# Arms of the second MoE in another order, without a copy for the last expert, and weight splits on two engines

## The chip, the cores and the metric

The kernel runs on one core of one Trainium2 chip. The metric is the time of one execution on the device in microseconds (us). Engines are named as in the profile: PE is TensorE (PEld its weight loads, PEldq the sequencer that issues them), DVE VectorE, ACT ScalarE, POOL GpSimd, SP SyncE.

## The reference

Three layers run one after the other: a local attention with pooled blocks (2 x 8 heads, 768 positions, 64 wide), a dense MoE with a gated activation (1536 tokens, 512 to 2048 to 512), and a second MoE with 8 experts, which the change concerns:

```python
def _moe2_ref(x, w_gate, w1, w2, capacity):      # capacity = 1536 // 8 * 2 = 384
    logits = x @ w_gate
    expert_idx = np.argmax(logits, axis=1)
    ...                                          # gate_w: softmax weight of that expert
    for i in range(N):                           # first come, first served
        e = expert_idx[i]
        if counts[e] < capacity:
            disp[e, counts[e]] = x[i]
            ...
    h = np.maximum(np.einsum('ecd,edf->ecf', disp, w1), 0.0)   # 512 -> 1024
    y = np.einsum('ecf,efd->ecd', h, w2)                       # 1024 -> 512
    ...                                          # out[i] = gate_w[i] * y[...] or 0
```

Which expert a token takes comes out of the data. For these inputs five of the eight experts have tokens: 878 (of which 384 are kept), 427 (384 kept), 168, 62 and 1. In blocks of 128 tokens that is 3, 3, 2, 1 and 1, ten blocks in all.

## The kernel before

[...]

**The order of the work** is written out by a small planner, `Plan`. Operations are added with an engine, a cost, a due time, and what they read and write; `emit` simulates the engines and writes each engine's instructions in the order that comes out. Among the operations that are ready, the one with the lowest rank goes first, where the rank is 0.67 times the due time less the operation's longest path to the end of the plan (`turn`, L113). One long plan covers everything up to the first block of the second MoE; it is searched with 1200 random variations of the ranks, scored by the planner's own simulation (`tries`, L116 to L125). The plans of the second MoE after that are made once, without a search.

**The experts** are sorted on the device by their number of blocks, the two fullest (of those counted early) first. The first expert's first block lies in the long plan, its second and third come after it. For the expert at place `i` (1, 2, ...) `body(i, nb)` writes the code. `nb` is that expert's number of blocks, a register that each engine reads from a small table (`get_nb`). There are two ways to do an expert's blocks:

- `add_blk`: one block of 128 tokens. First layer: 48 matmuls of 256 columns (L810), ReLU on ScalarE, transposes and splits; second layer: 8 steps of 3 matmuls of 512 columns (L822); scaling (`add_y`) and a scatter to the output by GpSimd (L844).
- `add_pair`: two blocks together (L859, L868), 144 matmuls. A third block, where there is one, follows by `add_blk`.

**While an expert is computed, the next one is prepared** (`more` and `then` in `body`): its token table is loaded (`add_tab`), its tokens are gathered (`add_gather`, L743), transposed and split (`add_prep`), and its weights are split (`add_splits`). The weights come as 8 pieces of 512 KB. Each piece is loaded by SP into a ring of six buffers (`add_stage`, L725), cast to the high part (`split_h`, L731 on ScalarE or L733 on VectorE) and subtracted to the low part (`split_l`, L737). The splits of expert `i + 1` free the ring for the last two pieces of expert `i + 1` and the first six of expert `i + 2`. Of the eight pieces `j`, VectorE casts 2 and 6 and ScalarE the others; GpSimd subtracts 1, 4 and 6 and VectorE the others. GpSimd's work and some of VectorE's take the plan's one `port` in turn.

**The code's shape.** All arms lie in each engine's instruction stream one behind the other, and every engine takes the branches for itself. `body(i)` tests first whether the next expert has a block (L1312). If so, the blocks of expert `i` follow with the preparation of the next, and then `body(i + 1)`, nested within. If not, a second copy of the blocks without any preparation stands in the Else arm, behind all the nested code. In each copy the test of `nb > 1` (L1299) falls through to the code for a pair, behind which the third block stands under `nb > 2` (L1302); the code for one block is the Else arm behind both.

Of the kernel before, what the change touches and what calls it, by code (L numbers as in the profile page):

```python
# [131 lines left out]
def fused_kernel(ctx, tc, qT, kT, vT, vp, w12, wg, wgT, mwe, consts, out, cap=384, dbg=None):  # L132
    nc = tc.nc
    PE, ACT, DVE, POOL, SP = nc.tensor, nc.scalar, nc.vector, nc.gpsimd, nc.sync
# [8 lines left out]
    E = mwe.shape[0]  # L143
# [42 lines left out]
    nblk = CAPR // 128  # L186
# [531 lines left out]
    def xg_at(p, b):  # L718
        return 2 * p + b if b < 2 else 4 + p

    def xs_at(p, b):
        return 2 * p + b % 2

    def stage(i, j, reg, eng=None):
        (eng or SP).dma_start(out=m2["raw"][(8 * i + j) % len(m2["raw"])],  # L725
                     in_=mwe[bass.ds(reg, 1), :, j, :].rearrange("o p f -> (o p) f"))

    def split_h(i, j, eng):
        r, h = m2["raw"][(8 * i + j) % len(m2["raw"])], m2["wh"][i % 2][j]
        if eng is ACT:  # L730
            ACT.activation(out=h, in_=r, func=AF.Copy)  # L731
        else:
            eng.tensor_copy(out=h, in_=r)  # L733

    def split_l(i, j, eng):
        r, h = m2["raw"][(8 * i + j) % len(m2["raw"])], m2["wh"][i % 2][j]
        eng.tensor_tensor(out=m2["wl"][i % 2][j], in0=r, in1=h.bitcast(F32), op=ALU.subtract)  # L737

    def load_tab(t, reg):
        SP.dma_start(out=tabs[t], in_=tab[bass.ds(reg * CAPR, CAPR), :].rearrange("(b p) o -> p (b o)", p=128))  # L740
# [7 lines left out]

    def add_stage(P, i, j, reg, due, eng="Q", r=()):
        P.add(eng, 1.46 if eng == "Q" else .06, due, lambda: stage(i, j, reg(), ENG.get(eng)), r=r,  # L750
              w=[("st", (8 * i + j) % 6)], lat=2.0 if eng == "Q" else 3.5)

    def add_split(P, i, j, due, new=False):
        he = "DVE" if j in (2, 6) else "ACT"
        le = "Pool" if j in (1, 4, 6) else "DVE"
        p, st = i % 2, ("st", (8 * i + j) % 6)

        def h():
            if new:
                wslot(p, j)  # L760
            split_h(i, j, ENG[he])
        hport = ["port"] * (he != "ACT")
        P.add(he, COST[he]["h"], due, h, r=[st], w=[("wh2", p, j)], acq=["wt"] * new + hport, rel=hport)
        P.add(le, COST[le]["l"], due + .5, lambda: split_l(i, j, ENG[le]), r=[st, ("wh2", p, j)], w=[("w", p, j)],
              acq=["port"], rel=["port"])

    def add_splits(P, i, due, gap, cur, nxt, new=False):
        for j in range(8):
            add_split(P, i, j, due + gap * j, new)
            if j < 2:  # L770
                add_stage(P, i, j + 6, cur, due + gap * j)
            elif nxt is not None:
                add_stage(P, i + 1, j - 2, nxt, due + gap * j)

    def add_tab(P, t, reg, due, r=()):
        P.add("Q", .2, due, lambda: load_tab(t, reg()), r=r, w=[("tab", t)])

    def add_gather(P, p, b, t, due, r=()):
        P.add("Pool", 1.04, due, lambda: gather(p, b, t), r=[("tab", t)] + list(r), w=[("xg", xg_at(p, b))], lat=2.5)
# [16 lines left out]
    def add_prep(P, p, b, i, due):  # L796
        g, x = xg_at(p, b), xs_at(p, b)
        add_T(P, lambda: m2["xg"][g], i, lambda: (m2["xh"][x], m2["xl"][x]), due, [("xg", g)], ("xs", x))

    def add_blk(P, p, b, t, due):  # L800
        g, x = xg_at(p, b), xs_at(p, b)

        def l1(j):
            o = m2["hb"][j // 2][:, (j % 2) * 256:(j % 2) * 256 + 256]
            w_h, w_l = m2["wh"][p][j], m2["wl"][p][j]
            n = 0
            for k in range(4):
                ks, ws = slice(k * 128, k * 128 + 128), slice(k * 256, k * 256 + 256)
                for x_, w_ in ((m2["xh"][x], w_h), (m2["xh"][x], w_l), (m2["xl"][x], w_h)):
                    PE.matmul(out=o, lhsT=x_[:, ks], rhs=w_[:, ws], start=n == 0, stop=n == 11)  # L810
                    n += 1

        def relu(i):
            ACT.activation(out=m2["ta"][i], in_=m2["hb"][i], func=AF.Relu)

        def l2(f):
            fs = slice((f % 4) * 128, (f % 4) * 128 + 128)
            g_h, g_l = m2["gh"][f // 4][:, fs], m2["gl"][f // 4][:, fs]
            j, ws = 4 + f // 2, slice((f % 2) * 512, (f % 2) * 512 + 512)
            w_h, w_l = m2["wh"][p][j], m2["wl"][p][j]  # L820
            for n, (g_, w_) in enumerate(((g_h, w_h), (g_h, w_l), (g_l, w_h))):
                PE.matmul(out=m2["acc"][b % 3], lhsT=g_, rhs=w_[:, ws], start=f == 0 and n == 0,  # L822
                          stop=f == 7 and n == 2)

        for j in range(4):
            P.add("PE", 1.43, due + 1.3 * j, lambda j=j: l1(j), r=[("w", p, j), ("xs", x)], w=[("hb", j // 2)])
        for i in range(2):
            P.add("ACT", .6, due + 2.6 * i + 2.6, lambda i=i: relu(i), r=[("hb", i)], w=[("ta", i)])
            add_T(P, lambda i=i: m2["ta"][i], i, lambda i=i: (m2["gh"][i], m2["gl"][i]), due + 2.6 * i + 3.1,
                  [("ta", i)], ("g2", i))  # L830
        for f in range(8):
            P.add("PE", .70, due + 5.2 + .7 * f, lambda f=f: l2(f),
                  r=[("g2", f // 4), ("g2", f // 4, "h"), ("w", p, 4 + f // 2)], w=[("ac", b % 3)])
        add_y(P, p, b, t, due + 11)
# [58 lines left out]
    def wslot(p, j):  # L893
        w = slot("w2", F32R)
        m2["wh"][p][j], m2["wl"][p][j] = w[:, 0, :], w[:, 1, :]

    with tc.manual_schedule():
# [40 lines left out]
        P = Plan(dict(wt=16, raw=3, port=1), dict(Q=1.5, ACT=3, DVE=3, Pool=3, PE=3))  # L938
# [35 lines left out]
        for u in range(NP):  # L974
            hp = u % HP
            (add if u < HP else both)(*(("ACT", .52) if u < HP else ("Pool", .7)), 21 + u + u // HP, lambda u=u: fill_v(u),
                r=[("vs", hp)] + ([("pk", u)] if u < HP else [("pv",)]), w=[("vf", u)])
# [10 lines left out]
        for u in range(NP):  # L988
            hp, b = u % HP, u // HP
# [222 lines left out]
    def get_id(i):  # L1212
        return SP.value_load(rint[0:1, i:i + 1], min_val=0, max_val=E - 1)

    def get_nb(i):
        return nc.values_load(rint[0:1, E + i:E + i + 1], min_val=0, max_val=nblk)
# [36 lines left out]
    with tc.If(m2["full"] > 0) as cmp:  # L1253
        with tc.manual_schedule():
            P = Plan(dict(port=1))
# [6 lines left out]
            nb = get_nb(0)  # L1262
        rest(0, True, nb, 2)
    with cmp.Else():
        with tc.manual_schedule():
            P = Plan(dict(port=1))
# [3 lines left out]
            nb = get_nb(0)  # L1270
        rest(0, False, nb, 1)

    def blocks(i, nb, more=lambda P: None, then=lambda P, due: None):
        p = i % 2

        def one(P):
            more(P)
            add_blk(P, p, 0, i % 4, 0)
            then(P, 9)

        def two(P):
            if nblk > 2:
                add_gather(P, p, 2, i % 4, 3)
            more(P)
            add_pair(P, p, i % 4, 0)
            if nblk > 2:
                add_prep(P, p, 2, 1, 17)
            then(P, 18)

        def plan(fn):  # L1290
            with tc.manual_schedule():
                P = Plan(dict(port=1), dict(ACT=1.9, Pool=1.6))
                fn(P)
                P.emit()

        if nblk == 1:
            plan(one)
            return
        with tc.If(nb > 1) as cmp:  # L1299
            plan(two)  # L1300
            if nblk > 2:
                with tc.If(nb > 2):  # L1302
                    plan(lambda P: add_blk(P, p, 2, i % 4, 0))
        with cmp.Else():
            plan(one)

    def body(i, nb):
        p = i % 2
        if i + 1 < E:
            with tc.manual_schedule():  # L1310
                nx = get_nb(i + 1)
            with tc.If(nx > 0) as cmp:  # L1312
                with tc.manual_schedule():
                    r = get_id(i + 1)
                    q = get_id(i + 2) if i + 2 < E else None

                def more(P):
                    add_tab(P, (i + 1) % 4, lambda: r, 0)
                    for b in range(min(nblk, 2)):
                        add_gather(P, 1 - p, b, (i + 1) % 4, 2 + b)  # L1320
                    add_splits(P, i + 1, 2, 1.2, lambda: r, None if q is None else lambda: q)

                def then(P, due):
                    for b in range(min(nblk, 2)):
                        add_prep(P, 1 - p, b, b, due)
                blocks(i, nb, more, then)
                body(i + 1, nx)
            with cmp.Else():
                blocks(i, nb)
        else:  # L1330
            blocks(i, nb)

    with tc.manual_schedule():
        nb = get_nb(1)
    body(1, nb)


# [77 lines left out]
```

## Time and profile before

| | |
|---|---|
| median of three runs (lowest, highest) | 549.02 us (547.86, 552.17) |
| the profiled execution's own time, its span | 551.83 us, 550.1 us |
| PE busy, DVE, ACT, POOL | 493.9 us (90% of the span), 356.7, 322.4, 112.7 |
| mean granted clock of TensorE | 0.953 |
| first matmul of the second expert after the first one's blocks | 432.55 us |
| last matmul | starts at 542.41 us, 0.40 us long |

Times in the profile are us from the start of the span. [...] A wait is the idle time of an engine just before an instruction, with the instruction or transfer that released it; "issue" stands where the profile shows nothing that was waited for. Branches are no busy time, but they have records with a start and a duration.

### The profile page before, as it was taken

The page shows a single profiled execution, that of the slowest core. Times are in us where ns is not written, and L with a number is a line of the kernel's source. Part 1 is how long each engine was busy: PE and PEld are TensorE (multiplying, and loading weights), DVE is VectorE, ACT ScalarE, POOL GpSimd, SP SyncE. Part 2 cuts the span into 40 slices and gives each one's busy share as a digit, 9 for nine tenths or more (in the row PEclk, how much of TensorE's full clock was granted, in tenths as well). Part 3 has the DMA queues.
Part 4 walks back from the last instruction along what each step waited for, and adds up shares of the span by engine and source line. Part 5 has one row for each costly group of instructions (what it writes and reads, how often), then busy time and mean ns, then how long its engine had stood idle before and what let it go on. Part 6 is the DMA issues. An engine that isn't in the chain of part 4 may idle for free.

```text
span 550.1 us, 9126 instructions
## 1 busy us (share of the span) xinstructions
PE 493.9 (90%) x3360; PEld 435.8 (79%) x3360; DVE 356.7 (65%) x705; ACT 322.4 (59%) x535; POOL 112.7 (20%) x110
## 2 busy tenths in 40 slices
PE   4977689998899999999999999969999999994754
PEld 3767588887788988988889989959888788884553
DVE  5479999999745896885885984445862373462400
ACT  2677788898367676666666655777523433532501
POOL 3450001010241000100101001141522351624400
PEclk9798699999899999999999999989999999996978
DMA  8999869521342532413533206844416672565520
GB/s 304 344 378 411 291 123 144 173 92 51 111 133 89 167 88 91 48 51 96 18 87 49 61 22 117 199 143 154 96 59 192 214 251 75 177 210 182 154 57 6
DMA packets 51587, 78.51 MB, mean 143 GB/s; under 512 B 15491, under 2 KB 34823, under 8 KB 49467
## 3 DMA queue, kind: packets, MB, share of 16 engines
q1 hardware_dynamic: 47850, 68.60, 45.0%
q0 software_dynamic: 2224, 5.47, 3.1%
q10 hardware_dynamic: 1440, 3.54, 1.8%
q8 instruction: 38, 0.62, 0.5%
q14 instruction: 35, 0.28, 0.2%
HBM read 67.39 MB, written 9.99 MB: 141 GB/s over the span
## 4 chain that ended last, share of the span: by engine, by line
PE 57%; DMA 17%; issue 9%; DVE 8%; ACT 5%; SPq 1%; POOL 1%; another core or an unknown queue 0%; POOLq 0%; ACTq 0%; DVEq 0%
PE h L520 18%; PE acc L557 16%; DMA out_dram<-tb,tabs 13%; PE av L452 4%; PE sc L379 4%; PE hb L810 3%; PE acc L822 2%; DMA xg<-x2d,tabs 2%; PE pt L428 2%; DVE wtmp L225 2%; PE avx L557 2%; DMA kraw<-in_kT_dram 1%; PE mx L557 1%; PE hb L859 1%; PE tps L784 1%
## 5 line engine op out<-in xcount | busy, mean ns | idle before, releaser
L520 PE MATMUL h<-xh,ws 128*128 128x256 f32 x768 | 147.1, 286 | 3.5 <-DVE ws L238 2.1
L520 PEld LDWEIGHTS h<-xh,ws 128*128 128x128 f32 x768 | 121.9, 190 | 5.7 <-DVE ws L238 2.3
L557 PE MATMUL acc<-ws,gh 128*128 128x512 f32 x320 | 106.4, 414 | 3.1 <-ACT gh L540 3.1
L520 PE MATMUL h<-xl,ws 128*128 128x256 f32 x384 | 108.8, 283 | 0.0
L520 PEld LDWEIGHTS h<-xl,ws 128*128 128x128 f32 x384 | 73.1, 190 | 0.5
L526 ACT ACTIVATE tA<-h 128x512 f32<-128x512 f32 x48 | 28.4, 594 | 74.3 <-PE h L520 74.3
L557 PEld LDWEIGHTS acc<-ws,gh 128*128 128x128 f32 x320 | 59.0, 194 | 15.4 <-ACT gh L540 3.5
L557 PE MATMUL acc<-ws,gl 128*128 128x512 f32 x160 | 64.8, 405 | 3.0 <-DVE gl L544 3.0
L810 PE MATMUL hb<-w,xh 128*128 128x256 f32 x192 | 39.4, 304 | 16.3 <-issue 11.7
L664 POOL DMA_INDIRECT tab<-toki,ix x12 | 14.1, 1174 | 173.9 <-DVE ix L657 129.8
L810 PEld LDWEIGHTS hb<-w,xh 128*128 128x128 f32 x192 | 32.9, 208 | 18.0 <-issue 17.7
L536 DVE TENSOR_TENSOR tA<-h,tA 128x512 f32<-128x512 f32 x48 | 31.3, 682 | 15.0 <-ACT tA L531 15.0
L557 PEld LDWEIGHTS acc<-ws,gl 128*128 128x128 f32 x160 | 30.9, 193 | 12.0 <-DVE gl L544 4.6
L791 DVE TENSOR_TENSOR gl<-tps,gh 128x512 fp32r<-128x512 f32 x12 | 8.3, 688 | 45.2 <-ACT gh L788 45.1
L544 DVE TENSOR_TENSOR gl<-tA,gh 128x1024 fp32r<-128x1024 f32 x24 | 32.1, 1340 | 7.6 <-PE mx L557 3.0
L607 DVE SCALAR_TENSOR_TENSOR dots<-x,wgb 128x512 f32<-128x512 f32 x48 | 33.4, 695 | 2.0 <-DMA wgb<-in_wgT_dram 1.2
L737 POOL TENSOR_TENSOR w<-mr,w 128x1024 fp32r<-128x1024 f32 x11 | 28.0, 2548 | 32.0 <-ACT w L731 24.2
L737 DVE TENSOR_TENSOR w<-mr,w 128x1024 fp32r<-128x1024 f32 x17 | 28.9, 1703 | 4.5 <-ACT w L731 4.4
L822 PE MATMUL acc<-w,gh 128*128 128x512 f32 x96 | 31.2, 406 | 0.0
L532 ACT ACT_TABLE_LOAD x24 | 30.8, 1283 | 0.4
L529 ACT ACT_TABLE_LOAD x24 | 30.8, 1283 | 0.4
L408 ACT ACTIVATE s<-s,nm 128x120 f32<-128x120 f32 x64 | 24.4, 384 | 9.2 <-POOL vz L358 8.4
(189 smaller groups left out, 1021.7 us busy)
## 6 DMA issues: line engine op xcount, KB each, us to landing
w<-in_w_dram SPq DMA_DIRECT2D x16, 1024.0 KB
mr<-in_mwe_dram SPq DMA_DIRECT2D x28, 512.0 KB
q<-in_qT_dram SPq DMA_DIRECT2D x16, 256.0 KB
kraw<-in_kT_dram SPq DMA_DIRECT2D x8, 400.0 KB
x2d<-x SPq DMA_DIRECT2D x6, 513.0 KB
kw<-in_kT_dram SPq DMA_DIRECT2D x16, 192.0 KB
vw<-in_vp_dram SPq DMA_DIRECT2D x16, 192.0 KB
out_dram<-zer SPq DMA_DIRECT2D x1, 3072.0 KB
```

The source lines that it names most:

```text
L408: ACT.activation(out=s[:, t, :], in_=ps[:, t, :], func=AF.Exp, bias=nm[:, t:t + 1], scale=0.125, accum_out=sm[:, t:t + 1])
L520: PE.matmul(out=o, lhsT=w_, rhs=x_[:, k, :], start=n == 0, stop=n == 3 * HP - 1)
L526: ACT.activation(out=tA[s][:, i * 512:i * 512 + 512], in_=hps[s, i], func=AF.Tanh, scale=0.5)
L529: ACT.preload_act_table_set("trig_and_small")
L532: ACT.preload_act_table_set("exp_and_others")
L536: DVE.tensor_tensor(out=t, in0=hps.pop((s, i)), in1=t, op=ALU.mult)
L544: (POOL if s in GLP else DVE).tensor_tensor(out=gl[s].rearrange("p a b -> p (a b)"), in0=tA.pop(s), in1=gh[s].bitcast(F32).rearrange("p a ...
L557: PE.matmul(out=acc[c][t], lhsT=g_, rhs=w_, start=(ft == 0 and n == 0), stop=(ft == NFT - 1 and n == 2))
L607: DVE.scalar_tensor_tensor(out=rt[c]["ps"], in0=rt[c]["x"][:, t, 0:DM], scalar=1.0, in1=wgb[i][:, j * DM:j * DM + DM], op0=ALU.mult, op1=A ...
L737: eng.tensor_tensor(out=m2["wl"][i % 2][j], in0=r, in1=h.bitcast(F32), op=ALU.subtract)
L810: PE.matmul(out=o, lhsT=x_[:, ks], rhs=w_[:, ws], start=n == 0, stop=n == 11)
L822: PE.matmul(out=m2["acc"][b % 3], lhsT=g_, rhs=w_[:, ws], start=f == 0 and n == 0, stop=f == 7 and n == 2)
```

## The change

Three things. First, every split casts on ScalarE and subtracts on VectorE; this holds for the first two experts too, whose splits are in the long plan. Second, `body` has one copy of the blocks, which always prepares the next expert (unless `i` is the eighth place); the test for a next expert comes behind the blocks. So the last expert that has tokens also prepares an expert without tokens. Third, in that copy the one-block code falls through, and the pair with the third block is the Else arm. Along with that, the one-block arm gathers and prepares one block of the next expert instead of two where `i` is 2 or more, and the due times are lower: 1 + b instead of 2 + b for the next expert's gathers, 4 instead of 9 for the prepares in the one-block arm, 13 instead of 18 in the pair, and 15 instead of 17 for the third block's.

```diff
--- before.py
+++ after.py
@@ -751,8 +751,7 @@
               w=[("st", (8 * i + j) % 6)], lat=2.0 if eng == "Q" else 3.5)
 
     def add_split(P, i, j, due, new=False):
-        he = "DVE" if j in (2, 6) else "ACT"
-        le = "Pool" if j in (1, 4, 6) else "DVE"
+        he, le = "ACT", "DVE"
         p, st = i % 2, ("st", (8 * i + j) % 6)
 
         def h():
@@ -1270,65 +1269,61 @@
             nb = get_nb(0)
         rest(0, False, nb, 1)
 
-    def blocks(i, nb, more=lambda P: None, then=lambda P, due: None):
+    def plan(fn):
+        with tc.manual_schedule():
+            P = Plan(dict(port=1), dict(ACT=1.9, Pool=1.6))
+            fn(P)
+            P.emit()
+
+    def body(i, nb):
         p = i % 2
+        ahead = min(nblk, 2 if i < 2 else 1)
+        nx = r = q = None
+        if i + 1 < E:
+            with tc.manual_schedule():
+                nx = get_nb(i + 1)
+                r = get_id(i + 1)
+                q = get_id(i + 2) if i + 2 < E else None
+
+        def more(P, n):
+            if nx is None:
+                return
+            add_tab(P, (i + 1) % 4, lambda: r, 0)
+            for b in range(n):
+                add_gather(P, 1 - p, b, (i + 1) % 4, 1 + b)
+            add_splits(P, i + 1, 2, 1.2, lambda: r, None if q is None else lambda: q)
+
+        def then(P, due, n):
+            for b in range(n if nx is not None else 0):
+                add_prep(P, 1 - p, b, b, due)
 
         def one(P):
-            more(P)
+            more(P, ahead)
             add_blk(P, p, 0, i % 4, 0)
-            then(P, 9)
+            then(P, 4, ahead)
 
         def two(P):
             if nblk > 2:
                 add_gather(P, p, 2, i % 4, 3)
-            more(P)
+            more(P, 2)
             add_pair(P, p, i % 4, 0)
             if nblk > 2:
-                add_prep(P, p, 2, 1, 17)
-            then(P, 18)
-
-        def plan(fn):
-            with tc.manual_schedule():
-                P = Plan(dict(port=1), dict(ACT=1.9, Pool=1.6))
-                fn(P)
-                P.emit()
+                add_prep(P, p, 2, 1, 15)
+            then(P, 13, 2)
 
         if nblk == 1:
             plan(one)
-            return
-        with tc.If(nb > 1) as cmp:
-            plan(two)
-            if nblk > 2:
-                with tc.If(nb > 2):
-                    plan(lambda P: add_blk(P, p, 2, i % 4, 0))
-        with cmp.Else():
-            plan(one)
-
-    def body(i, nb):
-        p = i % 2
-        if i + 1 < E:
-            with tc.manual_schedule():
-                nx = get_nb(i + 1)
-            with tc.If(nx > 0) as cmp:
-                with tc.manual_schedule():
-                    r = get_id(i + 1)
-                    q = get_id(i + 2) if i + 2 < E else None
-
-                def more(P):
-                    add_tab(P, (i + 1) % 4, lambda: r, 0)
-                    for b in range(min(nblk, 2)):
-                        add_gather(P, 1 - p, b, (i + 1) % 4, 2 + b)
-                    add_splits(P, i + 1, 2, 1.2, lambda: r, None if q is None else lambda: q)
-
-                def then(P, due):
-                    for b in range(min(nblk, 2)):
-                        add_prep(P, 1 - p, b, b, due)
-                blocks(i, nb, more, then)
+        else:
+            with tc.If(nb < 2) as cmp:
+                plan(one)
+            with cmp.Else():
+                plan(two)
+                if nblk > 2:
+                    with tc.If(nb > 2):
+                        plan(lambda P: add_blk(P, p, 2, i % 4, 0))
+        if nx is not None:
+            with tc.If(nx > 0):
                 body(i + 1, nx)
-            with cmp.Else():
-                blocks(i, nb)
-        else:
-            blocks(i, nb)
 
     with tc.manual_schedule():
         nb = get_nb(1)
```

## Rows read from the trace of the kernel before

**Rows 1.** Windows of three stages: each engine's busy us and instructions, clock, DMA share, GB/s.
```profile
0.00:405.00 405.00, 375.81 (x2628) 332.23 (x2629) 303.39 (x633) 274.68 (x460) 64.90 (x79) 0.96 0.52 141
...
432.50:495.00 62.50, 60.86 (x393) 54.05 (x392) 32.42 (x36) 26.40 (x43) 26.93 (x17) 1.00 0.57 178
495.00:528.50 33.50, 16.37 (x90) 14.14 (x88) 10.07 (x12) 10.42 (x14) 13.16 (x8) 0.80 0.54 160
```

**Rows 2.** Waits of TensorE from 380 us on: total us, times, longest us.
```profile
PE hb L810 <- issue: 11.7, 3, 8.5
PE hb L810 <- ACT w L731: 4.6, 1, 4.6
```

**Rows 3.** Timeline of TensorE in the last 50 us: start, duration, idle before and releaser.
```profile
499.82 0.76 PE L810 MATMUL hb<-w,xh 128*128 128x256 f32 x2 [4.58 <-ACT w L731]
...
504.49 0.58 PE L810 MATMUL hb<-w,xh 128*128 128x256 f32 x1 [2.83 <-issue]
...
512.87 0.65 PE L784 MATMUL tps<-ident,ta 128*128 128x128 f32 x4 [1.23 <-ACT ta L814]
...
528.55 0.77 PE L810 MATMUL hb<-w,xh 128*128 128x256 f32 x2 [8.54 <-issue]
```

**Rows 4.** Branches of TensorE's weight-load sequencer, by line: ns min/median/max, first and last start.
```profile
L1299 PEldq COMPARE_BRANCH  x1: 65/65/65, 430.6 to 430.6; - x1
...
L1302 PEldq COMPARE_BRANCH  x1: 286/286/286, 466.8 to 466.8; - x1
...
L1302 PEldq COMPARE_BRANCH  x2: 319/561/803, 492.4 to 495.4; - x2
...
L1299 PEldq COMPARE_BRANCH  x1: 2764/2764/2764, 496.9 to 496.9; - x1
...
L1312 PEldq COMPARE_BRANCH  x1: 5258/5258/5258, 517.1 to 517.1; - x1
...
L1299 PEldq COMPARE_BRANCH  x1: 6004/6004/6004, 522.4 to 522.4; - x1
...
L1299 PEldq COMPARE_BRANCH  x1: 3310/3310/3310, 539.6 to 539.6; - x1
```

**Rows 5.** Windows of four short stretches, with the columns of rows 1.
```profile
364.80:368.30 3.50, 3.48 (x11) 2.95 (x12) 0.69 (x1) 2.33 (x4) 0.22 (x1) 0.52 0.31 119
499.80:508.20 8.40, 5.54 (x24) 5.27 (x25) 0.34 (x1) 0.00 (x0) 4.38 (x4) 0.50 0.86 261
520.00:525.00 5.00, 0.01 (x1) 0.00 (x0) 1.97 (x3) 0.69 (x2) 1.19 (x1) 1.00 0.83 222
528.50:532.20 3.70, 3.65 (x18) 3.68 (x18) 0.00 (x0) 0.00 (x0) 0.00 (x0) 0.52 0.05 13
```

**Rows 6.** Casts and subtractions of the splits: ns min/median/max, first and last start.
```profile
L731 ACT ACTIVATE w<-mr x21: 1038/1059/1069, 352.3 to 514.1; 128x1024 fp32r<-128x1024 f32 x21
...
L737 DVE TENSOR_TENSOR w<-mr,w x17: 1209/1224/3577, 347.5 to 520.2; 128x1024 fp32r<-128x1024 f32 x17
L737 POOL TENSOR_TENSOR w<-mr,w x11: 2359/2404/3259, 354.9 to 515.7; 128x1024 fp32r<-128x1024 f32 x11
```

**Rows 7.** The gathers among the DMA issues: count, median us from issue to landing.
```profile
xg<-x2d,tabs POOLq DMA_INDIRECT x13, 3.9
```

**Rows 8.** Branches of SyncE and GpSimd, and the end of the program: columns as in rows 4.
```profile
L1299 SPq COMPARE_BRANCH  x2: 38/42/45, 528.9 to 531.8; - x2
...
L1299 POOLq COMPARE_BRANCH  x1: 38/38/38, 545.9 to 545.9; - x1
...
L1411 POOLq DRAIN  x3: 46/107/3007, 546.3 to 549.8; - x3
```

**Rows 9.** GpSimd from 350 to 358 us, and a wait of TensorE before 405 us.
```profile
354.90 2.40 POOL L737 TENSOR_TENSOR w<-mr,w 128x1024 fp32r<-128x1024 f32 x1 [14.06 <-ACT w L731]
357.47 1.79 POOL L743 DMA_INDIRECT xg<-x2d,tabs  x1 [0.16 <-issue]
...
PE tps L784 <- DMA xg<-x2d,tabs: 3.8, 1, 3.8
```

## The prediction

> **What bounds the kernel now.** I read the windows first, cut where the stages end. Until 405 us TensorE works on attention, the first MoE and the first block of the second MoE; it is busy for 375.8 of 405 us there, and for 60.9 of 62.5 us in the stretch of the two experts that run as pairs of blocks (432.5 to 495). From 495 to 528.5 it is busy for 16.4 of 33.5 us, at a mean clock of 0.80, and afterwards again nearly without a break [rows 1]. So TensorE is the bound all the way, and the loose time lies where the fourth expert and then the fifth begin.
>
> The waits of TensorE say what this loose time is: 11.7 us in three pieces in which it "waited for nothing that the profile shows", and 4.6 us set down to a ScalarE cast [rows 2]. The order in time places them: 4.58 us before the fourth expert's first matmul at 499.82, 2.83 us within that block, 8.54 us before the fifth's at 528.55 [rows 3]. The branch records of TensorE's weight-load sequencer explain them. A branch that falls through takes 0.065 us (430.6 us); an unconditional jump over the code for one block takes 0.29 (466.8). But the jump over the code of two blocks and the third (to the one-block arm, 496.9) takes 2.76; the two in a row by which the fifth expert gets to its code (first to the copy without a successor, 517.1, then to the one-block arm in it, 522.4) take 5.26 and 6.00; the last one, when all is quiet, 3.31 [rows 4]. 496.9 + 2.76 = 499.7 and 522.4 + 6.00 = 528.4: the first matmuls follow 0.1 us later. So the 4.58 us is a jump too, and not the cast that the waits name.
>
> Each hole costs again through the clock. [...] Busy time there is 5.54 and 3.65 us, of which half, 2.8 and 1.8, is lost. The two transitions thus cost A = 4.6 + 2.8 + 2.8 = 10.2 us and B = 8.5 + 1.8 = 10.3 us.
>
> **The change, part by part.** The profiled execution took 551.83 us, 1.7 more than its span and 2.8 above the median of 549.02. I make the sum in its microseconds and take it off the median.
>
> *A, into the fourth expert.* Before, TensorE's sequencer meets a jump over the third block (0.80, at 492.4), lands at 495.4 on a jump over the one-block code (0.32), and at 496.9 on the one of 2.76. After, only the jump over the third block is left; where it lands, the count is read and two branches fall through. Of the path to 499.82, 2.76 + 0.32 = 3.1 us goes, and the wait becomes 1.5 us. The second hole (2.83) is a wait for the code after the landing, while the DMA engines are 0.86 busy [rows 5]; whether it comes again depends on where the code's blocks lie, so between 0 and 2.83; I take 0.8. Clock: after the 1.23 us wait at 512.87 [rows 3] the matmuls kept the durations of full speed, while the 3.8 us wait before 364.8 [rows 9] cost 3.5 us of half speed [rows 5]; 1.5 us is nearer the first, so 0.5 of the possible 1.8. Left: 2.8, saved 7.4 (ends 4.1 and 10.2).
>
> *B, into the fifth.* Two far jumps become one, at the end of the one-block arm over the code of two blocks and the third; the test of the successor and the test of the count then fall through. Nearest price: 5.26, same place, same moment, DMA engines 0.83 busy from 520 to 525 [rows 5]; ends 2.76 and 6.00. Between the end of the jump at 495.4 and 496.9 lie 1.2 us, in which the next count is read. The jump comes ahead of that reading now, so it starts near 516 and ends at 521.3, and with the reading the first matmul is at 522.5 to 523 instead of 528.55. TensorE ended at 528.55 - 8.54 = 520.0, so 3.0 us of wait stays, with 1.8 of clock and 0.8 for the following code. Left 5.6, saved 4.7 (ends 1 and 10).
>
> *Jumps that are new.* The second and third experts now jump over the one-block code into their arm. For the third this replaces the jump of 0.29 over the same code at 466.8; for the second it is added at 430.6, where TensorE has work until 432.5. At 0.3 it is hidden; at 2.76 it would show 0.9, at 6.0 some 4. I take 0.3. [...]
>
> *Splits.* For each expert ScalarE goes from 6 casts to 8 at 1.06 us (6.4 to 8.5), VectorE from two casts and five subtractions to eight subtractions (8 x 1.22 = 9.8), and GpSimd loses three of 2.40 (7.2). VectorE's subtraction took up to 3.58 where GpSimd worked beside it [rows 6], so VectorE hardly loses. In the pair stage TensorE covers this: 62.5 us hold some 17 us of casts. I take 0.3 for casts that stand in front of a ReLU. In a one-block arm of some 14 us, casts, ReLUs and copies fill ScalarE for 12 to 13 us; the fourth expert already pays 1.23 for two casts in front [rows 3]. I add 0.5 there, and 1.7 for the fifth, which had no splits at all (0 to 3).
>
> *The fifth expert's new work.* It now prepares an expert with no tokens: one table, one gather, eight loads of 512 KB, eight splits, one transposition group. On TensorE those four transposes are paid by the second prepare that the fourth expert drops. The due time of the prepares, 4 for 9, moves their rank in the plan from 3.9 to 0.55 (0.67 x due less the 2.13 of their path), and second-layer step f ranks at -4.16 + 1.17 f: so their transposes move from behind the seventh of eight steps to behind the fifth, about 10.5 us into a block. A gather issued 4 to 5 us in and landing 3.9 us later [rows 7] is there by then: 0. At the end the span outlasts the last matmul by about 7 us, of which GpSimd's drain is 3.0 [rows 8]. GpSimd gets a second jump; its last one, at 545.9, stood 0.4 us ahead of the drain. SP is the risk: behind the fourth expert's loads its own jumps had it at 528.9 and 531.8, 8.9 and 11.8 us after the last matmul of that block [rows 8], and now the same loads lie in front of the end. They start sooner without GpSimd's splits. I take 1.2 (0 to 4).
>
> *The long plan before 405 us* holds the splits of the first two experts, and its order is searched anew at random. One stall there belongs to the change: TensorE waits 3.8 us for a gather, which GpSimd issued at 357.5, right behind a subtraction of 2.40 that is now gone [rows 9]; 2.4 of it and the clock's 1.7 could go, unless the new order takes it back. I take -1.5 (-5 to +4).
>
> Sum: -7.4 - 4.7 + 0.3 + 0.3 + 0.5 + 1.7 + 1.2 - 1.5 = -9.6, so 549.0 - 9.6 = 539.4 us.
>
> **The rivals.** *The number of jumps falls, their price does not.* What TensorE waits for is code behind data in the DMA engines (0.83 to 0.86 busy in both holes), and one jump at 6.00 with a second wait of 2.83 behind it does what two did. Then A saves 4.1, B 1: 549 - 5.1 + 4.0 - 1.5 = 546.4. For it: the 2.83 follows a jump that was already paid. Against: 11.3 us of B are two records that add up.
>
> *Slower: the new order of the long plan.* The search scores its own model, which knows nothing of a gather that lands late. TensorE idles 29.2 us before 405 [rows 1]. If a worse order adds two thirds of this, 19, the rest (-8.1 without the gain there) cannot carry it: 560. It decides from 13.6 us more idle time on, where slower by 1% begins. Against: the same search with as many tries has left only these 29.2 us, those before the first data arrived among them.
>
> *The end grows.* If SP and the fifth expert's loads set the end with 11.8 us after the last matmul where 7 stood, 4.8 instead of 1.2: 543.0, still faster or at the edge of no change.
>
> **How the numbers follow.** A measurement of this kernel can tell about 1%, 5.5 us. Forecast with its spread and the longer end: 0.70; jumps at their old price: 0.21; the worse plan: 0.09. Adding the ends of each term as independent gives -7 and +10 around 539.4; the range is 531 to 549.5, which takes in the second case and leaves out the third and the best corner. Faster 0.69, same 0.22, slower 0.09.
>
> **What would show it.** Between the third and fifth experts the branch records should hold one jump of TensorE over 2 us, not three; the waits without a cause fall from 11.7 to about 5 us; the half-speed stretch after the fourth expert's start is gone. GpSimd has no subtractions, VectorE none over 1.3 us. The fifth block gets a wait for a ReLU of 1 to 2 us. Wrong would make it: the first L810 matmul of the second MoE moved by more than 4 us either way (the plan), a jump of 5 us at 430 or 468, or an end more than 9 us behind the last matmul.

## The result, and the profile after

The changed kernel took 542.16 us (median of four runs, 540.21 to 544.11) against 550.56 of the kernel before beside it; the ratio is 0.987, with a 95% interval of 0.983 to 0.992. In a second session it was 0.988 (0.983 to 0.994). So it is 1.2 to 1.3% faster, 6 to 7 us by these ratios (the two medians lie 8.4 us apart), where 9.6 were forecast. The profiled execution took 540.21 us, 1.95 us below its median, the one of before 551.83, 1.3 above its own: these two flatter the change, and stages tell more than their totals. One execution of one experiment below (mixed splits, 547.72 us) was in a slower state of the chip, and no ratio or median here counts it.

The windows of the fourth and the fifth expert in the changed kernel, cut at the last matmuls of the third, the fourth and the fifth; columns as in rows 1:

```profile
495.10:510.50 15.40, 13.10 (x84) 11.31 (x84) 11.20 (x11) 11.15 (x14) 3.10 (x3) 1.00 0.71 223
510.50:527.30 16.80, 13.23 (x84) 11.25 (x84) 11.19 (x12) 11.14 (x14) 2.82 (x2) 1.00 0.89 290
```

In the 33.5 us in which TensorE was busy for half of the time at a clock of 0.80 [rows 1] there was one block and the way to the next; now 32.2 us (15.40 + 16.80) hold two blocks, at 1.00. TensorE's waits there (rows 3 after):

```profile
496.15 0.48 PE L809 MATMUL hb<-w,xh 128*128 128x256 f32 x2 [1.05 <-ACTq L1322]
503.75 0.66 PE L783 MATMUL tps<-ident,ta 128*128 128x128 f32 x4 [1.23 <-ACT ta L813]
512.69 0.48 PE L809 MATMUL hb<-w,xh 128*128 128x256 f32 x2 [2.22 <-issue]
520.23 0.66 PE L783 MATMUL tps<-ident,ta 128*128 128x128 f32 x4 [1.23 <-ACT ta L813]
```

The 4.58 us became 1.05, the 2.83 is gone, the 8.54 became 2.22, and the fifth block has got the ReLU wait of the fourth. The waits without a cause from 430 us on fall from 11.7 to 3.3 us in all. The branches of TensorE's weight-load sequencer (rows 4 after; L1317 is the test of one block and the jump over its Else arm, L1325 the test of a next expert):

```profile
L1317 PEldq COMPARE_BRANCH  x1: 2836/2836/2836, 428.1 to 428.1; - x1
...
L1317 PEldq COMPARE_BRANCH  x1: 333/333/333, 466.7 to 466.7; - x1
...
L1317 PEldq COMPARE_BRANCH  x2: 68/2076/4085, 507.8 to 512.5; - x2
...
L1317 PEldq COMPARE_BRANCH  x1: 5241/5241/5241, 524.6 to 524.6; - x1
L1325 PEldq COMPARE_BRANCH  x1: 4497/4497/4497, 530.3 to 530.3; - x1
```

Between the third and the fifth expert one jump over 2 us is left, 4.09 (the first of the two in its row). At the end there are two, 5.24 and 4.50, where one of 3.31 was [rows 4].

That a long jump waits for code is read from the same traces, in which one of the DMA queues is named "q8 instruction" (38 packets, 0.62 MB before, 36 and 0.59 MB after). From 425 us on, every branch record of this sequencer over 2 us, in all twelve profiles, overlaps a packet of 16 KB on this queue, and none of the jumps under 1 us does. The record ends 1.0 to 1.9 us behind the last such packet. The second hole of before, from 501.66 to 504.49, holds such a packet too (502.15 to 503.10).

### The profile page after: what moved, and what is told of

Same layout as the page of the kernel before. It is cut to its first block, busy times and chain, and to the rows that moved or that the text cites. A ratio compares the mean times of both kernels' runs of the same rounds, so it can differ in the third digit from the quotient of the medians.

```text
span 538.5 us, 9210 instructions
## 1 busy us (share of the span) xinstructions
PE 487.6 (91%) x3360; PEld 428.3 (80%) x3360; DVE 359.5 (67%) x718; ACT 339.7 (63%) x553; POOL 71.6 (13%) x95
## 5 line engine op out<-in xcount | busy, mean ns | idle before, releaser
L557 PE MATMUL acc<-ws,gh 128*128 128x512 f32 x320 | 104.4, 408 | 3.2 <-ACT gh L540 2.2
L557 PEld LDWEIGHTS acc<-ws,gh 128*128 128x128 f32 x320 | 57.9, 190 | 15.7 <-ACT gh L540 2.6
L737 DVE TENSOR_TENSOR w<-mr,w 128x1024 fp32r<-128x1024 f32 x32 | 38.4, 1220 | 18.5 <-ACT w L731 18.5
L731 ACT ACTIVATE w<-mr 128x1024 fp32r<-128x1024 f32 x32 | 32.8, 1057 | 9.5 <-issue 5.0
L809 PE MATMUL hb<-w,xh 128*128 128x256 f32 x192 | 35.1, 283 | 3.3 <-issue 2.2
L607 DVE SCALAR_TENSOR_TENSOR dots<-x,wgb 128x512 f32<-128x512 f32 x48 | 33.5, 697 | 1.0
L809 PEld LDWEIGHTS hb<-w,xh 128*128 128x128 f32 x192 | 29.6, 189 | 4.5 <-issue 4.1
L544 DVE TENSOR_TENSOR gl<-tA,gh 128x1024 fp32r<-128x1024 f32 x24 | 29.5, 1229 | 4.7 <-PE mx L557 3.7
L531 ACT ACTIVATE tA<-tA,hpi 128x1024 f32<-128x1024 f32 x24 | 27.6, 1152 | 0.8
## 6 DMA issues: line engine op xcount, KB each, us to landing
x2d<-x SPq DMA_DIRECT2D x6, 513.0 KB
```

Source lines behind the costliest of these rows:

```text
L544: (POOL if s in GLP else DVE).tensor_tensor(out=gl[s].rearrange("p a b -> p (a b)"), in0=tA.pop(s), in1=gh[s].bitcast(F32).rearrange("p a ...
L557: PE.matmul(out=acc[c][t], lhsT=g_, rhs=w_, start=(ft == 0 and n == 0), stop=(ft == NFT - 1 and n == 2))
L607: DVE.scalar_tensor_tensor(out=rt[c]["ps"], in0=rt[c]["x"][:, t, 0:DM], scalar=1.0, in1=wgb[i][:, j * DM:j * DM + DM], op0=ALU.mult, op1=A ...
```

## The experiments

For each profile I read five instants off TensorE's timeline: the second expert's first matmul, the last matmul of the third, the fourth and the fifth expert, and the end of the span. The table gives the stretches between them in us (pairs, A, B, tail), their sum, and the ratio of times to the kernel before with its 95% interval.

| | pairs | A | B | tail | sum | ratio |
|---|---|---|---|---|---|---|
| before | 62.7 | 24.8 | 22.8 | 7.3 | 117.6 | |
| changed | 64.1 | 15.4 | 16.8 | 11.2 | 107.6 | 0.987 (0.983 to 0.992) |
| changed, again | 64.1 | 15.3 | 18.4 | 13.0 | 110.8 | 0.988 (0.983 to 0.994) |
| new splits only | 64.0 | 23.8 | 22.5 | 7.2 | 117.5 | 1.002 (0.999 to 1.005) |
| new code only | 62.8 | 15.8 | 19.6 | 12.5 | 110.7 | 0.989 (0.985 to 0.993) |
| no last work | 64.1 | 15.3 | 14.8 | 9.6 | 103.9 | 0.985 (0.981 to 0.989) |
| no far loads | 64.1 | 15.3 | 14.6 | 9.2 | 103.3 | 0.977 (0.972 to 0.981) |
| old order | 64.0 | 23.5 | 15.5 | 11.3 | 114.2 | 1.000 (0.997 to 1.003) |
| copy back | 64.1 | 16.0 | 22.9 | 7.1 | 110.1 | 0.991 (0.988 to 0.994) |
| chain | 64.1 | 17.1 | 15.3 | 12.7 | 109.1 | 0.990 (0.987 to 0.994) |
| mixed splits | 62.8 | 15.3 | 16.9 | 10.7 | 105.7 | 0.989 (0.983 to 0.995) |
| last falls through | 62.8 | 15.9 | 12.6 | 8.5 | 99.8 | 0.968 (0.963 to 0.972) |

What lies before the pairs is not in the sum. It scatters from run to run: the second expert's first matmul came between 430.5 and 437.5 us in these profiles.

**New splits only.** Theories: the gain is the jumps, or it is the splits.

```diff
-        he = "DVE" if j in (2, 6) else "ACT"
-        le = "Pool" if j in (1, 4, 6) else "DVE"
+        he, le = "ACT", "DVE"
```

> Only the splits are moved to ScalarE and VectorE; the arms and the copy for the last expert are those of the kernel before. Theory J (the gain is the jumps): the three jumps of 2.8, 5 and 6 us stay, the long plan before 405 us gives about 1.6 us, the stage of the pairs takes about 1.4 back: 549 to 552 us against 550.6. Rival S (the gain is GpSimd's port given free and the long plan): 545 us or less.

550.26 us beside 548.63: no gain. The holes, now of 4.33, 1.70 and 7.56 us, stand where they stood; the pairs take 1.3 us more. Rival S fell.

**New code only**: the changed kernel with the old two lines of splits put back.

> Only the order of the arms and the copy for the last expert are changed, with their due times; the splits stay on three engines. Theory J: nearly the whole gain, 538 to 543 us, the waits before the fourth and fifth expert at 1 to 3 us, and the first matmul of the second expert at 432.5 us as in the kernel before. Rival S: 546 us or more.

544.03 us. The code alone carries the gain (0.989 against 0.987), and A is that of the changed kernel. B is 2.8 us longer than in the changed kernel's first profile and 1.2 longer than in its second, the tail 1.3 longer than in the first and 0.5 shorter than in the second: the splits' part there is not settled.

**No last work.**

```diff
-            if nx is None:
+            if nx is None or i == 4:
                 return
...
-            for b in range(n if nx is not None else 0):
+            for b in range(n if nx is not None and i != 4 else 0):
```

> The changed kernel, but the fifth expert prepares nothing for the sixth place, which has no tokens here (a kernel that would be wrong for inputs that use six experts). Theory L (the useless loads and splits hold up the last jumps and the end): the end comes 7 us after the last matmul instead of 11, and the 1.2 us wait for a ReLU in the fifth block goes: 5 us less, 537 us. Rival N (the end is set by two far jumps in place of one, whatever is loaded): at most 1.5 us less, 540.5 us or more.

541.74 us, which is N's time. By the stages both theories held half: the fifth block lost its ReLU wait and 2.0 us, and the tail lost 1.6 of the 3.9 us by which it had grown; the jumps behind the fifth block are still 3.82 and 4.30 us without any load, against 5.24 and 4.50. In this profile what lies before the pairs was the slowest of all (437.5 us), and so its time shows less than its stages; whether the other executions were as slow there is not on record.

**No far loads.**

```diff
-            add_splits(P, i + 1, 2, 1.2, lambda: r, None if q is None else lambda: q)
+            add_splits(P, i + 1, 2, 1.2, lambda: r, None if q is None or i in (3, 4) else lambda: q)
```

> The changed kernel without the loads of the six weight pieces for the sixth and seventh place, which the fourth and the fifth expert issue (no tokens there for these inputs; the splits of the sixth place run on what the buffers hold). The same jumps over the same code. Theory D (a far jump waits for code behind data in the DMA engines): the jump behind the fourth block goes from 4.1 to about 2.8 us, the two at the end from 5.2 and 4.5 to about 3.3; the end 8 us behind the last matmul; 538 us. Rival F (a jump costs by its distance): 4.1, 5.2 and 4.5 stay within 0.4, and the time within 1.5 us of 542.

537.33 us, theory D's time; its jump prices only in part:

```profile
L1317 PEldq COMPARE_BRANCH  x2: 68/1656/3245, 508.6 to 512.5; - x2
...
L1317 PEldq COMPARE_BRANCH  x1: 3701/3701/3701, 523.2 to 523.2; - x1
L1325 PEldq COMPARE_BRANCH  x2: 198/2270/4342, 527.4 to 532.1; - x2
```

The same jump behind the fourth block costs 3.25 us in this one profile, and 4.09 to 5.26 in the six that have its loads (changed 4.09, no last work 4.33, mixed splits 4.40, new code only 4.83, copy back 4.89, changed again 5.26); the wait before the fifth expert falls to 0.33. The last one of 4.34 stays. The DMA packets show where the difference lies: the 16 KB packet of the instruction queue starts 0.95 us behind this branch here (509.5), 1.5 us in the changed kernel (509.3), where the weight loads keep the DMA engines 0.93 busy (507.8 to 510.9), and 2.9 us in its second profile (511.6). So a far jump here costs 3.2 to 4.3 us without far loads, and behind the fourth block 0.8 to 2.0 more with them: its code comes later.

**Old order**, and **copy back**: each undoes one half of the new code (the second diff in outline).

```diff
-            with tc.If(nb < 2) as cmp:
-                plan(one)
-            with cmp.Else():
+            with tc.If(nb > 1) as cmp:
                 plan(two)
                 ...
+            with cmp.Else():
+                plan(one)
```

> The changed kernel with the old order of the arms: the pair falls through, the one-block code is the Else arm; still one copy. Theory O (the order of the arms saves what is lost before the fourth expert, the missing copy what is lost before the fifth): from the third expert's last matmul to the fourth's again 24 to 25 us instead of 15.4, from there to the fifth's last matmul 16 to 18 us; at the end one far jump instead of two, so about 2 us less there; 549 us, no gain over the kernel before. Rival M (the missing copy makes most of the gain, the order little): 545 us or less.

```diff
+        with tc.If(nx > 0) as last:
+            blocks()                  # the changed kernel's arms, with more and then
+            body(i + 1, nx)
+        with last.Else():
+            blocks()                  # the same arms without more and then
```

> The changed kernel with a second copy of the blocks, without any preparation, for the last expert, as in the kernel before; the arms in the new order. Theory O: two far jumps in a row before the fifth expert again, the wait there 5 to 7 us instead of 2.2 and half speed after it; the end again 7 to 8 us behind the last matmul instead of 11.2, and no wait for a ReLU in the fifth block: the two sides cancel, 541 to 544 us. Rival P (the second jump costs nothing because the first already hides it, so that the useless preparation is pure loss): 538 us or less. Rival Q (the missing copy is where the gain is): 546 us or more.

548.17 and 544.29 us: theory O held in both but for one point. With the old order A is 23.5 us again and nothing is gained, although the second jump into the fifth expert is gone (B 15.5): the tail of 11.3 and the pairs' 1.3 take their share. The point that failed is this tail: TensorE and GpSimd have one far jump there instead of two, and it is no shorter than the changed kernel's 11.2, so the number of jumps does not set it (what does, see *The end* below). The old order also has the lower due times and the dropped prepare; in A these alone gain no more than 0.3 us (23.5 for the 23.8 of new splits only). With the copy back, these two rows stand ahead of the fifth expert, and the wait there is 7.82 us with half speed behind it (a clock of 0.50 from 520.6 to 524.2), more than expected:

```profile
L1317 PEldq COMPARE_BRANCH  x1: 4885/4885/4885, 510.1 to 510.1; - x1
...
L1328 PEldq COMPARE_BRANCH  x1: 4876/4876/4876, 515.4 to 515.4; - x1
```

The tail is 7.1 in exchange. With the copy in place the order of the arms goes with 0.9% (the new splits in it), and the missing copy with 0.3 to 0.4% on top, which is within the intervals; without the new order the missing copy is worth nothing.

**Chain.** From the fourth expert (place 3) on, one-block code follows one-block code (in outline):

```diff
+        if i == 3:
+            with tc.If(nb < 2) as cmp:
+                plan(one)
+                with tc.If(nx > 0):
+                    body(i + 1, nx, True)      # one-block code only from here on
+            with cmp.Else():
+                ...
```

> The changed kernel; from the fourth place on, where the experts are sorted and none later has more blocks, the one-block code goes on into one-block code for the next places with no Else arm between. The jump behind the fourth expert's block is gone, nothing else. Theory O: the wait of 2.2 us before the fifth expert's first matmul is gone, at the end a jump out of the chain takes the place of the one over the Else arm: 540 us. Rival: the code behind still comes late (a wait of 2 us or more without a jump): 542 us.

The wait before the fifth expert is gone, as expected, and the time is 544.30 us: nothing gained. In its place TensorE waits for gathers inside both blocks, 1.16 and 0.96 us, and the jumps at the end are 5.44 and 4.66. The tail of 12.7 is set by SP this time: its drain (the engine's last step) starts at 541.3, GpSimd's at 535.1. Why the gathers come late was not tried. The first of these waits (start, duration, what it is, and the idle time before it):

```profile
511.48 0.66 PE L783 MATMUL tps<-ident,xg 128*128 128x128 f32 x4 [1.16 <-DMA xg<-x2d,tabs]
```

**Mixed splits.** Old splits up to place 3, new ones from place 4 on:

```diff
         he, le = "ACT", "DVE"
+        if i < 4:
+            he = "DVE" if j in (2, 6) else "ACT"
+            le = "Pool" if j in (1, 4, 6) else "DVE"
```

> The changed kernel with the old splits (VectorE and GpSimd too) for the experts at places 0 to 3 and the new ones from place 4 on. Theory O: from the second expert's first matmul to the third's last 62.7 us instead of 64.1, the fourth and the fifth as in the changed kernel (15.4 and 16.8 us): 541 us. Rival: the old splits cost in the pairs what they cost beside one block, and nothing is gained: 542 us or more.

The pairs are back at 62.8 us, A and B as in the changed kernel. The time, 540.91 us (median of five), is near the 541 expected, but its ratio of 0.989 is no better than the changed kernel's 0.987 and 0.988, with a wide interval: the gain of the pairs doesn't show in it.

**Last falls through.** Mixed splits, and in a chain from place 3 on (in outline):

```diff
+                with tc.If(nx < 1) as last:
+                    plan(one)                  # without more and then
+                with last.Else():
+                    plan(one)                  # with them
+                    body(i + 1, nx, True)
```

> A version for all inputs, put together from the runs before it: old splits for the experts at places 0 to 3, new ones after; from place 3 on a chain of one-block code in which the test for a next expert comes first, the block without any preparation falls through, and the block with preparation is the Else arm, followed by the next place. So the last expert has its own code again, but no far jump leads to it. Theory O, by stage against the changed kernel: pairs 62.8 us (64.1), to the fourth's last matmul 15.5 to 18 (15.4; one jump over one block's code is new), to the fifth's 12.5 to 13.5 (16.8), from there to the end 8.5 to 9.5 (11.2; no useless loads, still two far jumps): 4 to 6 us less, 536 to 538 us. Rival (each jump into code that has not just been run past costs 3 to 5 us, the short one too): the new jump shows as a wait of 3 us with half speed behind it, and the time is 541 us or more.

533.75 us beside 552.56 of the kernel before and 546.16 of the changed one in the same session; it beats both, by more than the 4 to 6 us expected. Its windows of the fourth and the fifth expert:

```profile
493.30:509.20 15.90, 13.03 (x86) 11.68 (x86) 11.11 (x11) 11.28 (x14) 2.60 (x3) 1.00 0.66 218
509.20:521.80 12.60, 12.55 (x81) 10.69 (x79) 1.49 (x3) 3.09 (x5) 1.00 (x1) 1.00 0.34 122
```

The fifth block fills its 12.6 us; the new short jump, over one block's code, cost 0.228 us, and the wait before the fourth block is 1.65 us where it was 1.05, at full speed behind it. At the end one jump of 3.61 and one of 0.19 are left, so the tail came out at the lower end.

**The changed kernel again.**

> The changed kernel once more, beside the version above. Theory O and its rivals alike: 540 to 544 us, 1 to 1.6% under the kernel before; stages as in its first profile to 0.3 us after the second expert's first matmul, whereas that matmul itself may start anywhere from 430 to 438 us.

546.16 us, above the 540 to 544 expected, but the kernel before was slower in that session too (552.56), and 1.16% under it is as expected. The stages were not within 0.3 us: the three far jumps took 5.26, 4.78 and 7.05 us, and the wait of 2.63 before the fifth expert, unlike that of 2.22, had reduced speed behind it (mean clock 0.71 from 514.8 to 518.4). The price of a far jump differs from run to run.

## Why the prediction was right, and where its terms were off

The likeliest case came true: faster by 1.2 to 1.3%, inside the range, by the jumps. That the sum came so near is in part luck: the two transitions gave more than forecast, and the end, the splits in the pairs and the long plan took it back. One of the signs that were to make it wrong did come, an end more than 9 us behind the last matmul (11.2, and 13.0 in the second profile); the other two did not (the first one-block matmul of the second MoE at 380.23 for 383.00, the jump at 428.1 at 2.84). Its terms, by the first profile of the changed kernel:

- *A*, with the added ReLU wait: 7.4 - 0.5 = 6.9 forecast, 9.4 measured. The wait was 1.05 for 1.5, neither the second hole nor half speed came (a clock of 1.00, for 0.50 before [rows 5]), and the ReLU wait stayed at 1.23. The wait was off by a misread row: of the two jumps of L1302 [rows 4], the one at 492.4 took 0.32 and the one that it lands on, at 495.4, 0.80, and I had them the other way round (row below, of before). With 2.76 + 0.80 off the path the same sum leaves 1.0.

```profile
L1302 PEldq COMPARE_BRANCH  x1: 803/803/803, 495.4 to 495.4; - x1
```

- *B*, with the fifth expert's splits: 4.7 - 1.7 = 3.0 forecast, 6.0 measured here and 4.4 in the second profile. The jump took 4.09 for 5.26 (5.26 in the second), the wait 2.22 for 3.0, and full speed stayed in the first (a clock of 1.00 from 512.6 to 516.2, for 0.52 behind the wait of before [rows 5]); the ReLU wait was 1.23 for 1.7. The 1.2 us between jump and count comes from the same misread row; it is 0.6 there.
- *New jumps*: 0.3 forecast, 0.29 measured (idle just before 430.95, ahead of the pairs) and 1.30 in the second profile, but not for the reason given. I priced the added jump at 0.3 by the row of 466.8; it took 2.84 (2.3 to 3.9 in the others), and TensorE's queued work hid most of it. A 16 KB packet of the instruction queue lies within it (428.3 to 429.5). The jump over nearly the same code at 466.7 (one prepare less) took 0.33 in the same trace, with no such packet. Both come 0.8 us behind another short jump (0.32 at 427.3, 0.18 at 465.9), the second after 12 us of straight code; what makes the difference was not tried.
- *Splits in the pairs*: 0.3 forecast, 1.4 measured: too small, and for casts, where I had VectorE hardly lose. VectorE's subtractions are even now (maximum 1.226 us, row below, against 3.577 [rows 6]), but TensorE waits twice 0.4 for a VectorE product, in every profile with the new splits there and in none with the old; that it stands in a longer queue is not shown. The rest is spread.

```profile
L737 DVE TENSOR_TENSOR w<-mr,w x32: 1214/1218/1226, 357.2 to 522.9; 128x1024 fp32r<-128x1024 f32 x32
```

- *The end*: 1.2 forecast (0 to 4), 3.9 measured, 5.7 in the second profile. This is the term that was most mis-sized, and for another reason than the two that I weighed, GpSimd's second jump (0.4 us) and SP. GpSimd's branches at 529.6 and 534.6 lie 5 us apart, but that is no jump: it runs semaphore instructions at 530.1 to 530.5, and then stands until 533.7, when its last scatter to the output has landed (the instruction's start follows the last of the scatter's 16 completions by 0.02 us). That scatter is issued 1.05 us behind the last matmul in every profile. From there it took 5.3 us to land for 2.3 before (the two rows of DMA issues below, after and before), and 7.1 in the second profile. So GpSimd's drain of 2.9 us, which ends last, began 7.4 us behind the last matmul, for 3.5 before.

```profile
L1325 POOLq EVENT_SEMAPHORE  x5: 17/43/43, 530.1 to 530.5; - x5
L1325 POOLq COMPARE_BRANCH  x2: 38/44/50, 529.6 to 534.6; - x2
L1325 POOLq INC_SWDGE_SEM  x1: 865/865/865, 533.7 to 533.7; - x1
...
L1406 POOLq DRAIN  x3: 46/107/2922, 534.7 to 538.2; - x3
```

```profile
out_dram<-tb,tabs POOLq DMA_INDIRECT x1, 5.3
out_dram<-tb,tabs POOLq DMA_INDIRECT x1, 2.3
```

The other profiles agree. The scatter lands in 5.4 us with the old order and in 2.1 with the copy back, and the tails are 11.3 and 7.1; without the last work or the far loads it lands in 3.8 and 3.3, and the tails are 9.6 and 9.2. So 3.0 of the 3.9 us is the scatter, and the rest is the semaphore instruction of 0.865 us, which stood ahead of the landing before and stands behind it now. Of the 3.0 us, 1.5 to 2.0 goes with the loads or the last work; why the scatter still takes longer than 2.3 without them stays open.

- *The long plan*: -1.5 forecast. The stall named there did go: the gather is issued at 349.17, and the 3.8 us wait [rows 9] with it. But the order was drawn anew throughout, and TensorE's waits for the first MoE's split weights grew in that order from 2.9 to 9.4 us (a row of GpSimd's timeline, and two of the waits up to 405 us after the change; the same two sums before are 2.1 and 0.8):

```profile
349.17 0.99 POOL L743 DMA_INDIRECT xg<-x2d,tabs  x1 [9.59 <-issue]
```

```profile
PE h L520 <- DVE ws L238: 5.4, 3, 2.8
...
PE h L520 <- ACT ws L234: 4.0, 1, 4.0
```

In the first profile the second expert starts 1.6 us earlier, which looks like the forecast, but that is scatter: its first matmul comes at 432.8 us in the median of the eight profiles with the new splits there, and at 431.4 in that of the four with the old ones. New splits alone, with its 117.5 us of stages against 117.6 and its ratio of 1.002, also puts the new long plan 1 us above the old one, but within the interval. So the gain of 1.5 did not come; if the slower rival's mechanism acted, it was small.

Summed by the stages of the first profile: -9.4 - 6.0 + 1.4 + 3.9 = -10.1 (-6.8 for the second), and about +1 before them, against a measured 6 to 8 us. The first rival, jumps at their old price, fell for A (old order against changed: 8.1 us) and for B, which gave 6.0 and 4.4 us with the splits where it had 1 without them. The price of the one jump that stayed, 4.1 and 5.3 us in the two profiles, is not far from the old 5.3 and 6.0; the number of jumps made the gain. The third rival's longer end did come, nearly at its size (3.9 and 5.7 for 4.8 us), though GpSimd and not SP sets it.

## What to carry to other kernels

Count the taken far jumps on the path of the engine that bounds, price each by its branch record (2.8 to 6.0 us in the kernel before), and put the arm that runs when nothing is left to hide a jump where it falls through; an arm entered while the bounding engine still has queued work can stand behind it (of 2.84 and 3.86 us, 0.29 and 1.30 showed here). A copy of code is no loss in itself: what counts is whether the case that ends the program reaches it without a far jump, and what loads without a receiver are in flight when the last result is written (B was 12.6 us with the copy falling through and 22.9 with it behind two far jumps; the last scatter landed in 5.3 us with such loads and in 3.3 without). A long time between two branch records of an engine need not be a jump (the 5 us on GpSimd here were not): look at what it waited for in between. And a change to one operation's engine inside a randomly searched plan redraws the whole plan, so measure it apart.

## What was not expected of the hardware

A far jump costs more with loads in flight: 3.25 us in the one profile without them, 4.09 to 5.26 in the six with them, for the same code, and the trace's instruction packets start 0.95 us behind the branch there and 1.5 and 2.9 us in two of the others. The last scatter pays for loads too: 3.3 us from issue to landing without far loads, 5.3 and 7.1 with them. A wait of 2.22 us left TensorE at full speed (a granted clock of 1.00 from 512.6 to 516.2); one of 2.63 us in another execution of the same kernel had a mean clock of 0.71 behind it (514.8 to 518.4; half speed, 0.50, from 516.3 to 519.7), one of 2.68 in new code only 0.58 (513.0 to 516.6), and one of 7.82 in copy back 0.50 (520.6 to 526.0). And the wait list named a ScalarE cast for the wait of 4.58 us, which ends 0.2 us behind the end of a jump: the branch records say it, the releaser doesn't.
